# Gated mix of a recurrent memory transformer and a channel MLP: seven deferred tiles, a root of third order, and the first tile's projections behind the last block

## The chip, the cores and the metric

The kernel runs on one core of one Trainium2 chip. The metric is the time of one execution in device microseconds; the median of three runs is 767.43 us (767.12 to 767.94). The profile is of one further execution, with a trace of every instruction.

## The reference

The output mixes two branches of the same input x (2048 tokens of 512, bf16) with a gate per token.

```python
def _A_ref(x, mem0, Wq, Wk, Wv, Wo, seg_len):      # recurrent memory attention
    ...
    mem = mem0                                      # 8 memory tokens
    for s in range(n_seg):                          # 64 segments of 32 tokens
        xs = x[:, s * seg_len:(s + 1) * seg_len, :].copy()
        h = jnp.concatenate([mem, xs], axis=1)
        q = jnp.einsum('btd,dhe->bhte', h, Wq)      # 32 heads of 128
        k = jnp.einsum('btd,dhe->bhte', h, Wk)
        v = jnp.einsum('btd,dhe->bhte', h, Wv)
        ...                                         # masked softmax of q k, times v
        o = jnp.einsum('bhte,hed->btd', o, Wo)
        mem = o[:, :M, :].copy()                    # the next segment needs it
        outs.append(o[:, M:, :])
    return jnp.concatenate(outs, axis=1)

def _B_ref(x, w1, b1, w2, b2):                      # F = 1376
    y = _layernorm(x, axis=-1)
    h = _gelu(jnp.einsum('bsd,df->bsf', y, w1) + b1)
    return jnp.einsum('bsf,fd->bsd', h, w2) + b2

g = _sigmoid((x * gate_w).sum(-1, keepdims=True))
return g * _A_ref(...) + (1 - g) * _B_ref(...)
```

## The kernel before

The 2048 tokens are 16 tiles (T) of 128 tokens; a tile is four segments, and a segment is one step (s = 4 T + si, 64 steps). The kernel has two phases. Every engine runs its instructions in the order in which the program text issues them; there is no scheduler in between (the region is under a manual schedule), so the text's order is each queue's order. Loads of data are DMAs issued from a queue: most from SP (`nc.sync`), a few from ScalarE (`nc.scalar`) and GpSimd (`nc.gpsimd`).

**First phase, the MLP.** It runs over 8 blocks of two tiles. A block has 11 units (fc), one for each 128 columns of F. `a_mm` (L464) computes one unit: four matmuls of 256 columns into bank SbF or W in turn, and a Gelu on ScalarE with the bias `b1_sb` into `hTm`. `b_mm` (L471) follows two units later (LAG) and multiplies the unit by w2 into the output bank of each tile, one 512-column matmul per tile. `prep` (L422) normalizes the next block's two tiles on VectorE; blocks after the first take the inverse root from `rsqrt` (L410), a bit trick with three Newton rounds on [128 x 2] values. `prep_tr` (L443) transposes the normalized tiles through X1 and X2. `gates` (L455) makes the gate and its complement `omg`, by which the finished block is scaled while it is evicted (`ct_out`, L493) and stored in DRAM (`c_dr`). While this goes on, the attention's weights arrive: `loads` (L351) issues two pieces of Wv, Wq or Wk in each of blocks 0 to 5, and Wo in block 6.

The tiles in `DEF` (L67) are deferred: their Gelu result is not multiplied by w2 here. `spill` (L484) writes it to DRAM (`h_dr`) in two pieces, and the second phase reads it back.

The start of the phase: 13 matmuls on an identity (`warm`, L519), the first two tiles' statistics, their transposes, two more such matmuls, the transpose of the bias (L529) through bank W with its copy to `b1_sb`, and then the units. In the last block `first` (L511) is spread between the units 5, 7 and 9: it projects the last 8 tokens of each segment of tile 0 to Q, K and V, in six parts of 16 matmuls each on quarter-width tiles (`left_qk`, `left_v`), through X1, X2 and U[0].

**Second phase, the steps.** A step projects 32 rows (24 tokens of its segment and the 8 memory rows) to Q, K and V (L127, L146), computes scores (`scores`), exponentials, the products with V (`av`, L289 and L294), and one pass of Wo for the rows of the step (`wo_pass`, L158), out of which `new_mem` (L728) takes the next memory. The last 8 tokens of each segment ("left") are projected a tile ahead as filler: `side` (L615) returns a generator of such work for each step, and `run(n)` and a few single calls put its items into the step's text where TensorE would wait. An item is four quarter-width matmuls of 512 columns. For the last tile there is no next tile, so `side` is empty there but for step 62.

The deferred tiles are another filler: `mlp_halves` (L653) reads one spilled unit `hm` and multiplies it by w2 in two halves of four quarter-width matmuls of 256 columns into bank W; two halves stand in each step (L805 and L814), and step 2 has seven units more. `hm_load` (L633) issues the load of a unit on SP, four ahead, into five buffers; it is called at the second half of a unit. `hm_load4` loads four units in one DMA, at step 2.

The softmax's normalization of the rows goes through DRAM: `recip_x` (L694) writes reciprocals to `r_dr` on SP and reads them back broadcast as `Rb` on SP. GpSimd's `x_norm` (L707) multiplies by Rb in the next step and writes UT, which `wo_pass` of that step reads.

At the border of the phases the tiles of the second phase (UT, QT, KT, E and others) take over the memory of the first, so their first writers wait for the last readers of what was there, the spills of hTm among them.

Of the kernel before, what the change touches and what calls it, by code (L numbers as in the profile page):

```python
# [10 lines left out]
BF16 = mybir.dt.bfloat16  # L11
I32 = mybir.dt.int32
ACTF = mybir.ActivationFunctionType
ALU = mybir.AluOpType
# [9 lines left out]
RSQRT_SEED = 0x5F3759DF  # L24
# [3 lines left out]
def kernel(ctx, tc, A_x, A_mem0, A_Wq, A_Wk, A_Wv, A_Wo, A_seg_len, B_x, B_w1, B_b1, B_w2, B_b2, gate_w, out):  # L28
# [38 lines left out]
    DEF = (1, 3, 5, 9, 11, 13)  # L67
# [232 lines left out]
    with tc.tile_pool(name="mlpw", bufs=1) as mlpw, \  # L300
# [35 lines left out]
        nc.sync.dma_start(w1_sb[:, :, F0:F1], w1v[:, :, F0:F1])  # L336
        nc.sync.dma_start(w1_sb[:, :, F1:F], w1v[:, :, F1:F])
        nc.gpsimd.dma_start(gw_bc[:], gate_w.partition_broadcast(P))
        nc.sync.dma_start(w2_sb[:, H2:FC - 1, :], B_w2[H2 * P:(FC - 1) * P, :].rearrange("(fc p) d -> p fc d", p=P))
# [70 lines left out]
        def rsqrt(y, v, n):  # L410
            i1 = msmall.tile([P, n], I32, tag="i1", name="i1")
            nc.vector.tensor_scalar(out=i1[:], in0=v.bitcast(I32), scalar1=1, scalar2=None, op0=ALU.logical_shift_right)
            nc.vector.tensor_scalar(out=y.bitcast(I32), in0=i1[:], scalar1=-1, scalar2=RSQRT_SEED, op0=ALU.mult, op1=ALU.add)
            for _ in range(3):
                t = msmall.tile([P, n], FP32, tag="nt", name="nt")
                nc.vector.tensor_tensor(out=t[:], in0=y, in1=y, op=ALU.mult)
                nc.vector.scalar_tensor_tensor(out=t[:], in0=t[:], scalar=-0.5, in1=v, op0=ALU.mult, op1=ALU.mult)
                nc.vector.scalar_tensor_tensor(out=y, in0=t[:], scalar=1.5, in1=y, op0=ALU.add, op1=ALU.mult)
# [3 lines left out]
        def prep(blk):  # L422
            mv = msmall.tile([P, TB, nc.vector.BN_AGGR_DIM], FP32, tag="mv", name="mv")
            ve = msmall.tile([P, TB], FP32, tag="ve", name="ve")
            rs = msmall.tile([P, TB], FP32, tag="rs", name="rs")
            for tt in range(TB):
                st = msmall.tile([P, nc.vector.BN_STATS_DIM], FP32, tag="st", name="st")
                nc.vector.bn_stats(out=st[:], in_=xts[blk * TB + tt][:])
                nc.vector.bn_aggr(out=mv[:, tt, :], in_=st[:])
            nc.vector.tensor_scalar(out=ve[:], in0=mv[:, :, 1], scalar1=LN_EPS, scalar2=None, op0=ALU.add)  # L430
            if blk == 0:
                nc.scalar.activation(out=rs[:], in_=ve[:], func=ACTF.Sqrt)
                nc.scalar.activation(out=dummy[:], in_=ident[:, 0:1], func=ACTF.Gelu_apprx_tanh)
                nc.vector.reciprocal(out=rs[:], in_=rs[:])
            else:
                rsqrt(rs[:], ve[:], TB)
            for tt in range(TB):
                T = blk * TB + tt
                ys[T] = mwork.tile([P, Dm], BF16, tag="y", name="y")
                nc.vector.tensor_scalar(out=ys[T][:], in0=xts[T][:], scalar1=mv[:, tt, 0:1], scalar2=rs[:, tt:tt + 1], op0=ALU.subtract, op1=ALU.mult)  # L440
            yTs[blk] = mwork.tile([P, KC, TB * P], BF16, tag="yT", name="yT")
# [13 lines left out]
        def gates(blk):  # L455
            t0, t1 = blk * TB, blk * TB + TB
            nc.scalar.activation(out=th[:, t0:t1], in_=z_all[:, t0:t1], func=ACTF.Tanh, scale=0.5)
            nc.vector.tensor_scalar(out=g_all[:, t0:t1], in0=th[:, t0:t1], scalar1=0.5, scalar2=0.5, op0=ALU.mult, op1=ALU.add)
# [5 lines left out]
        def a_mm(blk, fc):  # L464
            rows = min(P, F - fc * P)
            hp = (SbF, W)[(blk * FC + fc) % 2]
            for kc in range(KC):
                nc.tensor.matmul(hp[:rows, 0:TB * P], lhsT=w1_sb[:, kc, fc * P:fc * P + rows], rhs=yTs[blk][:, kc, :], start=(kc == 0), stop=(kc == KC - 1))  # L468
            nc.scalar.activation(out=hTm[blk % 2][:rows, fc, :], in_=hp[:rows, 0:TB * P], func=ACTF.Gelu_apprx_tanh, bias=b1_sb[:rows, fc:fc + 1], scale=1.0)
# [41 lines left out]
        def first():  # L511
            bks = (X1, X2, U[0], X1, X2, U[0])
# [11 lines left out]
        b1p = W[:].bitcast(BF16)[:, 0:FC]  # L524
# [3 lines left out]
        warm(2)  # L528
        nc.tensor.transpose(b1p, b1r[:], ident[:FC, :FC])  # L529
        nc.vector.tensor_copy(out=b1_sb[:], in_=b1p)  # L530
# [3 lines left out]
        for n, (blk, fc) in enumerate(units):  # L534
# [33 lines left out]
            elif fc >= 1:  # L568
                if fc == 2:
                    spill(blk - 1, 6, FC)  # L570
                if fc == 1:
                    side0 = first()
                if fc == 3:
                    gates(blk)
                for _ in range((0, 0, 0, 0, 0, 8, 0, 8, 0, 8, 0)[fc]):
                    next(side0, None)
                    flush(act_q, 9)
                    flush(dve_q, 9)
        for n in range(len(units) - LAG, len(units)):
            b_mm(*units[n])  # L580
        for _ in side0:
            flush(act_q, 9)
            flush(dve_q, 9)
# [69 lines left out]
    def mlp_halves():  # L653
        while hms:
            T, fc, hm, n = hms.pop(0)
            for h in range(2):
# [4 lines left out]
                if h == 1:  # L661
                    hm_load(n)
# [9 lines left out]

    hm_load(4)
# [20 lines left out]
    def recip_x(s):  # L694
# [4 lines left out]
        nc.sync.dma_start(r_dr[s % 2][:], R[:, 8 * NG:RW])  # L699
        nc.sync.dma_start(Rb[:].rearrange("p r e -> p (r e)"), r_dr[s % 2][:].rearrange("r e -> (r e)").partition_broadcast(P))  # L700
# [33 lines left out]
    for s in range(nseg):  # L734
# [18 lines left out]
        if s == 2:  # L753
            hm_load4()
# [49 lines left out]
        if not last:  # L804
            next(mlp, None)  # L805
# [8 lines left out]
        next(mlp, None)  # L814
# [200 lines left out]
```

## Time and profile before

| what | us |
|---|---|
| median of three runs | 767.43 |
| the profiled execution's own time | 767.13 |
| its span, first to last instruction | 765.4 |
| TensorE matmuls busy | 744.7 (97%) |
| TensorE weight loads busy | 423.4 (55%) |
| ScalarE busy | 537.1 (70%) |
| VectorE busy | 401.0 (52%) |
| GpSimd busy | 275.1 (36%) |

The granted TensorE clock is 0.998 over the span. The first phase ends and step 0 begins at 86 us; the rest are the 64 steps and a short tail.

How to read the rows: an engine is PE (TensorE), PEld (its weight loads), ACT (ScalarE), DVE (VectorE), POOL (GpSimd) or SP (SyncE); a trailing q means the engine's sequencer, which issues DMAs. L127 is a line of the kernel. "out<-in" names tiles, xN counts instructions that are merged into the row. In a timeline a row has its start in us from the span's start, its length, and in brackets the idle time of the engine before it and what ended it. A matmul's length is that from its issue to its modelled end; matmuls overlap, so the distance from start to start is what one costs. A list of waits has the engine and line that waited, what released it, the total in us, how often, and the longest. A row of stretches has the stretch, its length, busy time and count for PE, PEld, DVE, ACT and POOL, then the granted clock, the mean busy share of the 16 DMA engines, and GB/s.

### The profile page before, as it was taken

Reading aid. Unit: us, or ns where it says so; the run is one execution under the profiler, and the core shown is the slowest. Engines: PE = TensorE matmul, PEld = TensorE weight load, DVE = VectorE, ACT = ScalarE, POOL = GpSimd, SP = SyncE. Lnnn points to the kernel's source line nnn. Section 1 sums busy time; section 2 is a strip of 40 time slices with the busy share of each in tenths; the row PEclk is TensorE's granted clock in tenths of the full one; section 3 lists DMA queues with packets and bytes.
Section 4 is the critical chain, followed back from the end, with each engine's and each line's share of the span. In section 5 each row is a group of like instructions: output and inputs, shape, how many; then the busy total and the mean of one; then the engine's idle time right before and its main releaser. Section 6 shows DMA issues by size and latency. Waiting matters only on the chain.

```text
span 765.4 us, 44786 instructions
## 1 busy us (share of the span) xinstructions
PE 744.7 (97%) x19624; PEld 423.4 (55%) x19635; DVE 401.0 (52%) x1434; ACT 537.1 (70%) x1625; POOL 275.1 (36%) x517
## 2 busy tenths in 40 slices
PE   8999999999999999999999999999999999999997
PEld 5666455556555555655555655555555555555553
DVE  5876454545555544645455545445454555445444
ACT  4766676777777777777777777777777777677663
POOL 4001133344433334342444333343433444333441
PEclk9999999999999999999999999999999999999999
DMA  8999423212132322222121324222222213222211
GB/s 276 335 305 314 138 76 87 71 59 76 58 94 74 91 66 59 74 83 83 60 78 56 94 66 95 69 56 76 82 78 72 73 56 93 64 83 69 73 57 49
DMA packets 71994, 74.96 MB, mean 98 GB/s; under 512 B 39401, under 2 KB 61906, under 8 KB 70258
## 3 DMA queue, kind: packets, MB, share of 16 engines
q1 hardware_dynamic: 70354, 69.96, 30.1%
q8 instruction: 155, 2.54, 1.4%
q0 software_dynamic: 496, 1.18, 0.5%
q10 hardware_dynamic: 944, 0.92, 0.4%
q14 instruction: 45, 0.37, 0.2%
HBM read 59.13 MB, written 6.62 MB: 86 GB/s over the span
## 4 chain that ended last, share of the span: by engine, by line
PE 93%; DVE 3%; DMA 2%; issue 1%; ACT 1%; SPq 0%; DVEq 0%; ACTq 0%
PE U L127 33%; PE X L158 19%; PE X L146 16%; PE X L127 4%; PE U L289 3%; PE W L468 2%; PE U L475 2%; PE W L659 2%; PE U L146 2%; PE SbF L468 2%; PE U L265 1%; DMA w_sb<-in_B_w_dram 1%; PE U L728 1%; PE SbF L265 1%; PE SbF L685 1%
## 5 line engine op out<-in xcount | busy, mean ns | idle before, releaser
L712 POOL TENSOR_TENSOR UT<-XR,Rb 128x384 bf16<-128x384 bf16 x126 | 140.3, 1137 | 302.0 <-DMA Rb<-r_dr 234.0
L132 ACT CAST Tb<-U 128x512 bf16<-128x512 f32 x288 | 169.0, 587 | 81.7 <-PE U L127 79.1
L127 PEld LDWEIGHTS <-hT 128*32 128x32 bf16 x4096 | 109.5, 96 | 98.7 <-DVE hT L730 8.2
L146 PE MATMUL X<-Wv_sb,hT 128*32 128x512 bf16 x2048 | 144.1, 378 | 0.1
L127 PE MATMUL U<-Wq_sb,hT 128*32 128x512 bf16 x2048 | 137.1, 381 | 0.1
L127 PE MATMUL U<-Wk_sb,hT 128*32 128x512 bf16 x2048 | 133.5, 379 | 0.0
L158 PE MATMUL X<-Wo_sb,UT 128*32 128x512 bf16 x2016 | 122.7, 380 | 1.5 <-ACT UT L819 0.8
L730 DVE CAST hT<-U 128x8 bf16<-128x8 f32 x126 | 21.0, 167 | 168.3 <-PE U L728 126.1
L790 ACT CAST V<-X 128x256 bf16<-128x256 f32 x256 | 88.7, 372 | 16.4 <-PE X L146 3.5
L136 DVE STREAM_TRANSPOSE QT<-Tb 128x256 f32<-128x256 f32 x128 | 56.6, 442 | 73.2 <-ACT Tb L132 72.8
L158 PEld LDWEIGHTS <-UT 128*32 128x32 bf16 x2080 | 56.5, 96 | 60.7 <-issue 17.8
L691 ACT CAST XR<-U 128x256 bf16<-128x256 f32 x252 | 78.4, 433 | 0.0
L719 ACT CAST w<-X 128x128 bf16<-128x128 f32 x189 | 44.7, 309 | 43.6 <-PE X L158 43.6
L136 DVE STREAM_TRANSPOSE KT<-Tb 128x256 f32<-128x256 f32 x128 | 57.0, 445 | 31.1 <-ACT Tb L132 23.2
L712 POOL TENSOR_TENSOR UL<-XR,Rb 128x128 bf16<-128x128 bf16 x126 | 60.5, 504 | 0.0
L146 PEld LDWEIGHTS <-hT 128*32 128x32 bf16 x2048 | 47.1, 94 | 20.5 <-issue 0.2
L704 POOL TENSOR_TENSOR racc<-racc,R 128x72 f32<-128x72 f32 x63 | 21.3, 337 | 102.3 <-DVE R L702 82.1
L819 ACT CAST UT<-U 128x64 bf16<-128x64 f32 x252 | 35.3, 226 | 28.9 <-PE U L294 28.9
L468 PEld LDWEIGHTS <-w_sb 128*128 128x128 bf16 (+1 forms) x352 | 33.3, 100 | 18.6 <-issue 5.5
L773 ACT ACTIVATE E<-U 128x64 bf16<-128x64 f32 (+1 forms) x128 | 35.0, 273 | 11.3 <-PE U L269 11.2
L728 PEld LDWEIGHTS <-w 128*32 128x32 bf16 x1008 | 23.7, 93 | 31.9 <-ACT w L719 25.3
L127 PE MATMUL U<-Wk_sb,GL 128*32 128x512 bf16 x496 | 39.9, 377 | 0.0
(169 smaller groups left out, 1233.3 us busy)
## 6 DMA issues: line engine op xcount, KB each, us to landing
Rb<-r_dr SPq DMA_DIRECT2D x63, 512.0 KB, 4.0
Wv_sb<-in_A_Wv_dram SPq DMA_DIRECT2D x4, 1024.0 KB, 7.4
Wq_sb<-in_A_Wq_dram SPq DMA_DIRECT2D x4, 1024.0 KB, 8.2
Wk_sb<-in_A_Wk_dram SPq DMA_DIRECT2D x4, 1024.0 KB, 8.6
Wo_sb<-in_A_Wo_dram SPq DMA_DIRECT2D x4, 1024.0 KB, 11.1
VP<-VL SPq DMA_DIRECT2D x64, 64.0 KB, 3.3
c<-c_dr SPq DMA_DIRECT2D x16, 128.0 KB, 2.7
hm<-h_dr SPq DMA_DIRECT2D x62, 32.0 KB, 3.3
```

Source lines behind the costliest of these rows:

```text
L127: nc.tensor.matmul(bk[32 * j:32 * j + 32, :], lhsT=G[:, kc, :], rhs=W5[t][:, kc, h0:h1, j, :], start=(kc == 0), stop=(kc == KC - 1), tile_ ...
L132: nc.scalar.copy(out=Tb[:], in_=bk.rearrange("p (a b e) -> p a e b", a=8, b=2))
L136: nc.vector.transpose(out=dst[:, 8 * hf:8 * hf + 8, c0:c0 + 32, :].rearrange("p a r b -> p a (r b)").bitcast(FP32), in_=Tb[:].rearrange("p ...
L146: nc.tensor.matmul(bk[32 * j:32 * j + 32, :], lhsT=G[:, kc, :], rhs=Wv5[:, kc, 4 * vb:4 * vb + 4, j, :], start=(kc == 0), stop=(kc == KC - ...
L158: nc.tensor.matmul(bk[32 * c:32 * c + 32, :], lhsT=U_[:, j, i, :], rhs=Wo_sb[:, 4 * i + j, :], start=(n == 0), stop=(n == NW - 1), tile_po ...
L468: nc.tensor.matmul(hp[:rows, 0:TB * P], lhsT=w1_sb[:, kc, fc * P:fc * P + rows], rhs=yTs[blk][:, kc, :], start=(kc == 0), stop=(kc == KC - 1))
L691: nc.scalar.copy(out=XR[:, j], in_=U[j][:, 0:NG * 40].rearrange("p (i q) -> p i q", q=40)[:, :, 0:32])
L712: nc.gpsimd.tensor_tensor(out=out[:, :, 4 * h:4 * h + 4, o:o + b - a], in0=XR[:, :, 4 * h:4 * h + 4, a:b], in1=Rb[:, h, :, :, a:b], op=ALU ...
L719: nc.scalar.copy(out=w[:, a:b], in_=bk[:, a:b])
L773: nc.scalar.activation(out=E[:, 4 * i2:4 * i2 + 4, c], in_=Sb[i2][:, :, c], func=ACTF.Exp, scale=scale)
L790: nc.scalar.copy(out=V[:, i0:i0 + 2, :].rearrange("p i e -> p (i e)"), in_=(X1, X2)[vb][:, 256 * h:256 * h + 256])
L819: nc.scalar.copy(out=UT[s % 2][:, j, :, 0:M], in_=U[j][:, 0:NG * 40].rearrange("p (i q) -> p i q", q=40)[:, :, 32:40])
```

## The change

- `DEF` gets tile 15. Its Gelu result is spilled in the last block (two more spills on SP), its eleven 512-column matmuls of `b_mm` go, and its 11 units join the filler: `side` gives `mlp_units(4)` in steps 60 and 61, `hm_load4` is called at step 60 too, step 0 has no halves any more, and step 2 has eight units instead of seven.
- `hm_load` is no longer called at the second half of a unit. The number owed is counted, and `recip_x` issues the loads between the write of r_dr and the read of Rb.
- The root has two rounds, one of three and one of four instructions, with other constants; a scale is folded into the addition of epsilon.
- `gates` makes only `omg` in each block; `g_all` is made once, in the last block.
- `first` comes behind the last unit of the last block, in three portions of eight items, with the two lagging `b_mm` calls behind the first portion. It uses U[1] beside X1, X2 and U[0].
- The second piece of w1 is issued ahead of x tiles 2 and 3. The second piece of w2 moves from ScalarE's queue to SP's, behind these. Twelve matmuls instead of 13 and one instead of two are issued at the start, and the bias transpose and its copy move behind the matmuls of the first unit.

```diff
-RSQRT_SEED = 0x5F3759DF
+RSQRT_SEED, RSQRT_A, RSQRT_B = 0x5F1FFFF9, 2.38924456, 0.703952253
+RSQRT_K = 0.375 * RSQRT_B
...
-    DEF = (1, 3, 5, 9, 11, 13)
+    DEF = (1, 3, 5, 9, 11, 13, 15)
...
-        NWARM = 13
+        NWARM = 12
         H1, H2, F1 = 3, 6, 7 * P
-        for a, b in ((0, H1), (H1, H2)):
-            nc.scalar.dma_start(w2_sb[:, a:b, :], B_w2[a * P:b * P, :].rearrange("(fc p) d -> p fc d", p=P))
+        def ld_w2(eng, a, b):
+            eng.dma_start(w2_sb[:, a:b, :], B_w2[a * P:b * P, :].rearrange("(fc p) d -> p fc d", p=P))
+        ld_w2(nc.scalar, 0, H1)
+        nc.sync.dma_start(w1_sb[:, :, F0:F1], w1v[:, :, F0:F1])
         ld_x(2)
         ld_x(3)
-        nc.sync.dma_start(w1_sb[:, :, F0:F1], w1v[:, :, F0:F1])
+        ld_w2(nc.sync, H1, H2)
         nc.sync.dma_start(w1_sb[:, :, F1:F], w1v[:, :, F1:F])
...
-            for _ in range(3):
+            for c, a in ((-1.0, RSQRT_A), (-RSQRT_B * RSQRT_B, 5.0)):
                 t = msmall.tile([P, n], FP32, tag="nt", name="nt")
                 nc.vector.tensor_tensor(out=t[:], in0=y, in1=y, op=ALU.mult)
-                nc.vector.scalar_tensor_tensor(out=t[:], in0=t[:], scalar=-0.5, in1=v, op0=ALU.mult, op1=ALU.mult)
-                nc.vector.scalar_tensor_tensor(out=y, in0=t[:], scalar=1.5, in1=y, op0=ALU.add, op1=ALU.mult)
+                nc.vector.scalar_tensor_tensor(out=t[:], in0=t[:], scalar=c, in1=v, op0=ALU.mult, op1=ALU.mult)
+                if a == 5.0:
+                    nc.vector.scalar_tensor_tensor(out=t[:], in0=t[:], scalar=10.0 / 3.0, in1=t[:], op0=ALU.add, op1=ALU.mult)
+                nc.vector.scalar_tensor_tensor(out=y, in0=t[:], scalar=a, in1=y, op0=ALU.add, op1=ALU.mult)
...
-            nc.vector.tensor_scalar(out=g_all[:, t0:t1], in0=th[:, t0:t1], scalar1=0.5, scalar2=0.5, op0=ALU.mult, op1=ALU.add)
+            if blk == NBLK - 1:
+                nc.vector.tensor_scalar(out=g_all[:], in0=th[:], scalar1=0.5, scalar2=0.5, op0=ALU.mult, op1=ALU.add)
...
+            if blk == 0 and fc == 0:
+                b1p = W[:].bitcast(BF16)[:, 0:FC]
+                nc.tensor.transpose(b1p, b1r[:], ident[:FC, :FC])
+                nc.vector.tensor_copy(out=b1_sb[:], in_=b1p)
...
-            bks = (X1, X2, U[0], X1, X2, U[0])
+            bks = (X1, X2, U[0], U[1], X1, X2)
...
-                if fc == 1:
-                    side0 = first()
                 if fc == 3:
                     gates(blk)
-                for _ in range((0, 0, 0, 0, 0, 8, 0, 8, 0, 8, 0)[fc]):
-                    next(side0, None)
-                    flush(act_q, 9)
-                    flush(dve_q, 9)
-        for n in range(len(units) - LAG, len(units)):
-            b_mm(*units[n])
-        for _ in side0:
-            flush(act_q, 9)
-            flush(dve_q, 9)
+                if fc == 7:
+                    spill(blk, 0, 6)
+        spill(NBLK - 1, 6, FC)
+        side0 = first()
+        for n in range(3):
+            if n == 1:
+                for m in range(len(units) - LAG, len(units)):
+                    b_mm(*units[m])
+            for _ in range(8):
+                next(side0, None)
+                flush(act_q, 9)
+                flush(dve_q, 9)
...
-            gens = [wo_left(T - 1, X1) if T >= 1 else mlp_units(7)]
-        elif T + 1 < NT:
+            gens = [wo_left(T - 1, X1) if T >= 1 else mlp_units(8)]
+        elif T + 1 == NT:
+            gens = [mlp_units(4)] if si < 2 else []
+        else:
...
-                    hm_load(n)
+                    owed[0] += n
...
         nc.sync.dma_start(r_dr[s % 2][:], R[:, 8 * NG:RW])
+        hm_load(owed[0])
+        owed[0] = 0
         nc.sync.dma_start(Rb[:].rearrange("p r e -> p (r e)"), r_dr[s % 2][:].rearrange("r e -> (r e)").partition_broadcast(P))
...
-        if s == 2:
+        if s in (2, (NT - 1) * SPT):
             hm_load4()
...
         if not last:
-            next(mlp, None)
+            if s:
+                next(mlp, None)
...
         run(W1)
-        next(mlp, None)
+        if s:
+            next(mlp, None)
```

More of the change, by code (lines that the diff above doesn't have):

```diff
@@ L429, in prep @@
                 nc.vector.bn_aggr(out=mv[:, tt, :], in_=st[:])
[L430 removed]
+            nc.vector.tensor_scalar(out=ve[:], in0=mv[:, :, 1], scalar1=LN_EPS, scalar2=1.0 if blk == 0 else 1.0 / (RSQRT_K * RSQRT_K), op0=ALU.add, op1=ALU.mult)
             if blk == 0:
@@ L527 @@
             prep_tr(0, tt)
-        warm(2)
-        nc.tensor.transpose(b1p, b1r[:], ident[:FC, :FC])
-        nc.vector.tensor_copy(out=b1_sb[:], in_=b1p)
+        warm(1)
         side0 = iter(())
```

4 lines of the change are left out of this document (2 added, 2 removed).

## The prediction

> **What bounds the kernel now.** The page comes first: its span, the shares of the chain that ended last, and one queue.
>
> ```profile
> span 765.4 us, 44786 instructions
> ...
> PE 744.7 (97%) x19624; PEld 423.4 (55%) x19635; DVE 401.0 (52%) x1434; ACT 537.1 (70%) x1625; POOL 275.1 (36%) x517
> ...
> q8 instruction: 155, 2.54, 1.4%
> ...
> PE 93%; DVE 3%; DMA 2%; issue 1%; ACT 1%; SPq 0%; DVEq 0%; ACTq 0%
> ```
>
> The chain is 93% TensorE, so time is won by taking instructions from TensorE or by ending a wait of TensorE, and nowhere else. Its waits, longest first (us in total, times, longest):
>
> ```profile
> PE U L289 <- issue: 4.1, 10, 0.6
> ...
> PE W L468 <- ACT hTm L469: 1.4, 2, 1.0
> PE W L659 <- DMA hm<-h_dr: 1.2, 1, 1.2
> ...
> PE SbF L468 <- ACT hTm L469: 0.7, 2, 0.5
> PE W L468 <- DMA w_sb<-in_B_w_dram: 0.6, 1, 0.6
> PE X L447 <- DVE y L440: 0.5, 1, 0.5
> ```
>
> Four of these are what the change touches: the hm wait, the w_sb wait and the wait of a transpose for y (L447). The chain in order of time (start, length) then tells a step's length, because each L127 row opens one step.
>
> ```profile
> 84.72 1.30 PE U L475 x6
> 86.01 2.73 PE U L127 x48
> ...
> 97.65 3.69 PE U L127 x68
> ...
> 108.02 3.55 PE U L127 x64
> ...
> 705.69 3.55 PE U L127 x64
> ...
> 715.92 3.55 PE U L127 x64
> ...
> 726.14 3.51 PE U L127 x64
> ...
> 736.30 3.51 PE U L127 x64
> ```
>
> Step 0 takes 97.65 - 86.01 = 11.6 us, step 1 10.4. Steps 59, 60 and 61 take 10.23, 10.22 and 10.16. Step 59 still carries the 32 matmuls of the next tile's V; steps 60 and 61 carry no such filler and are no shorter. So the last tile's steps are set by their own chain of engines and have room for about 32 matmuls (8 x 0.217 us = 1.7 us of TensorE). One full-width 512-column matmul costs 1.30 / 6 = 0.217 us, and four quarter-width ones side by side cost the same.
>
> **The change part by part.** The sum is made against the profiled execution: span 765.4, its time 767.13, so 1.7 lie around the span. The runs' median, 767.43, is 0.3 above it.
>
> *Start.* The second piece of w1 is issued ahead of the x tiles, the second piece of w2 moves from ScalarE's queue to SP's behind them, two warming matmuls go, and the bias transpose moves behind the first unit. From the timeline (start, length, engine, line, what, idle time before and its releaser):
>
> ```profile
> 2.69 0.48 SPq L336 DMA_DIRECT2D w_sb<-in_B_w_dram  x1
> ...
> 7.56 0.76 DVE L448 COPY yT<-X 128x512 bf16<-128x512 bf16 x2 [0.71 <-PE X L447]
> ...
> 8.11 0.18 PE L529 MATMUL W<-ident,b1r 11*128 11x11 bf16 x1
> ...
> 8.37 0.60 PE L468 MATMUL SbF<-yT,w_sb 128*128 128x256 bf16 x4
> ...
> 9.44 0.47 ACT L469 ACTIVATE hTm<-W,b_sb 128x256 bf16<-128x256 f32 x1
> ...
> 9.96 0.38 PE L475 MATMUL U<-w_sb,hTm 128*128 128x512 bf16 x1
> ...
> 10.99 0.61 PE L468 MATMUL W<-yT,w_sb 128*128 128x256 bf16 x4 [0.65 <-DMA w_sb<-in_B_w_dram]
> ```
>
> Unit 3 waits until 10.99 for the w1 piece issued at 2.69. Its two other conditions are met by 10.18 (9.96 + 0.217, and the Gelu from bank W ends at 9.91). The missing warming matmul lets the transposes and unit 0 start some 0.4 earlier. But unit 1 writes bank W, through which the bias transpose now passes after unit 0 (transpose, semaphore, copy: 8.11 to about 8.5, 0.4 us), so unit 1 stays near 8.8. What is left is the load: two x tiles and 384 KB fewer are ahead of it, more than the 0.8 us it is late. I take -0.85; the ends are 0 (it lands as late as now) and -0.95. The pieces pushed back (x tiles, w2) are needed later; if one is late it eats into this term.
>
> *Root and gates.* Two of eleven small VectorE instructions go from each root (3 x 3 + 2 becomes 3 + 4 + 2), and one of two in the gates of seven blocks. The timeline where block 6 ends:
>
> ```profile
> 62.58 0.17 DVE L458 TENSOR_SCALAR g_all<-th 128x2 f32<-128x2 f32 x1 [0.27 <-ACT th L457]
> ...
> 62.66 0.16 DVE L459 TENSOR_SCALAR omg<-th 128x2 f32<-128x2 f32 x1
> ...
> 67.14 0.16 DVE L418 SCALAR_TENSOR_TENSOR rs<-nt,rs 128x2 f32<-128x2 f32 x1
> ...
> 67.33 0.73 DVE L440 TENSOR_SCALAR y<-xt,mv,rs 128x512 bf16<-128x512 bf16 x2
> ...
> 68.20 0.38 PE L447 MATMUL X<-ident,y 128*128 128x128 bf16 x4 [0.49 <-DVE hT L506]
> ```
>
> One root instruction takes 0.19 from start to start (67.14 to 67.33), so y comes 0.39 sooner; that matters only where a transpose waits, in two blocks with 0.5 each (the L447 row of the list of waits, and the 0.49 at 68.20): -0.8 (0 to -1.0). A gate instruction costs 0.08 (62.58 to 62.66). The omg behind it releases the scaled eviction on ScalarE, which holds up the Gelus, and for these TensorE waits 1.4 + 0.7 us in four places: 4 x 0.08 = -0.3 (0 to -0.6). In the other blocks both are hidden by TensorE's own work.
>
> *Tile 15 deferred.* Eleven 512-column matmuls leave the last block: 11 x 0.217 = -2.4. With one output matmul per unit instead of two, the last block becomes like the other deferred ones, which wait for a Gelu near their third unit (2.1 / 4 = 0.5 each): +0.4. The floor is -1.9, and -2.4 is the ceiling. The first tile's projections stay 24 groups of four; they only move behind the last block, where the Gelu tail and the Exp table load are covered by their 5 us.
>
> Added on SP: two spills of tile 15 (352 KB), behind the Wo loads and ahead of the VP load, the ct write, the hm loads and the first r_dr write. The last of them is awaited by the memsets of UT and the first write of QT. Rows of the timeline there, of two stretches, and of the issues (KB, us to landing):
>
> ```profile
> 86.12 1.42 POOL L598 MEMSET UT<- 128x768 bf16 x2 [12.74 <-PE U L475]
> ...
> 87.48 0.42 POOL L248 COPY QT<-QL 128x128 f32<-128x128 f32 x1
> ...
> 89.41 0.27 PE L265 MATMUL SbF<-QT,KT 128*32 128x40 bf16 x16
> ```
>
> ```profile
> 78.00:82.00 4.00, 3.95 (x47) 1.97 (x46) 1.09 (x3) 2.15 (x5) 0.00 (x0) 1.00 1.08 339
> 82.00:86.00 4.00, 4.00 (x47) 1.78 (x50) 1.25 (x4) 2.82 (x5) 0.00 (x0) 1.00 0.06 16
> ```
>
> ```profile
> h_dr<-hTm SPq DMA_DIRECT2D x2, 160.0 KB, 7.9
> ```
>
> The queues are full until 82 (share 1.08) and then empty (0.06); a spill behind Wo took 7.9 us. By the terms so far step 0 starts 3.95 earlier, near 82.0, and its scores need QT 3.4 later (89.41 - 86.01), at 85.4. If the transfers end as late as now, the spills end at 82 + 352 KB / 339 GB/s = 83.0, and QT follows 1.9 later (memsets and copy, 86.12 to 87.90, and a semaphore), at 84.9: covered by 0.5. At half that rate it is 86.0 and step 0 waits 0.6; at a third, 1.6. I take 0, since what stands ahead of Wo's issue moves forward too; ends 0 and +1.6.
>
> *hm.* Step 0 loses its two output halves and with them the wait: -1.2, to about the 10.4 of step 1. The eleven units of tile 15 add 22 halves of 0.11: one unit to step 2 (an empty place there), one to step 59, ten to steps 60 and 61, whose room is 1.7 us each: +0.2, and at most +2.4 if no place is empty. Their loads are issued between the r_dr write and the Rb load; see the fourth rival.
>
> *Pauses before L289.* TensorE pauses ten times, 4.1 us, with no releaser. There are 155 instruction fetches for 19,624 + 19,635 TensorE instructions, one per 253 (the second and third row of the page), so such a pause should fall where a fetch comes late in the dense run of small matmuls. Fewer instructions ahead of the loop shift where the fetches fall in every step. Direction unknown; ends -2 and +2 (half of the 4.1); I take +0.4, since steps 0 and 60 become dense enough to pause too. The Trainium skill ("Runtime: NRT & Kernel Launch", "Instruction fetch mechanics") says that blocks of 256 instructions are fetched ahead and that crossing one is mostly hidden. By that this term would be 0 and the time 0.4 less; the ten pauses speak against "hidden" here.
>
> Sum: -0.85 - 0.8 - 0.3 - 2.4 + 0.4 - 1.2 + 0.2 + 0.4 = -4.55. The profiled time becomes 762.6, and 0.3 more for a median of runs: 762.9.
>
> **The rivals.**
> First, step 0 waits for tile 15's spill: for it the full queues until 82, against it the half microsecond of cover. +1.6: 764.5.
> Second, the fetches fall worse in all 56 middle steps: +2, 764.9.
> Third, the front does not shorten: the start gives 0, the root's waits return behind another VectorE instruction, and only 1.9 + 1.2 remain less 0.6 for the steps: 767.4 - 2.5 = 764.9.
> Fourth, slower. In every step the hm load now stands on SP between r_dr and Rb. The timelines of GpSimd, TensorE and SP in step 58:
>
> ```profile
> 697.43 2.23 POOL L712 TENSOR_TENSOR UT<-XR,Rb 128x384 bf16<-128x384 bf16 x2 [4.39 <-DMA Rb<-r_dr]
> ```
>
> ```profile
> 702.72 1.91 PE L158 MATMUL X<-Wo_sb,UT 128*32 128x512 bf16 x32
> ```
>
> ```profile
> 703.07 0.46 SPq L699 DMA_DIRECT2D r_dr<-R  x1
> 704.68 0.32 SPq L700 DMA_DIRECT2D Rb<-r_dr  x1
> ```
>
> GpSimd waits for Rb, and UT is ready at 699.7 for a use at 702.7: 3.0 of slack; 1.6 lie between r_dr and Rb. An hm issue that is held up more than 4.6 us decides; at 5 us, 56 steps x 0.4 = 22 us, 785. Against it: each load takes a slot that an earlier step has read.
>
> **How the numbers follow.** Forecast 0.66, first rival 0.13, second 0.10, third 0.07, fourth 0.04. The forecast's own range is 761.5 to 764; 760.9 takes in a luckier fetch pattern, 765.2 the first three rivals. A measurement of this kernel tells 0.2% (1.5 us) from no change: faster is below 765.9. The first four cases, 0.96 together, lie there; of these I give 0.08 to no change and 0.01 to slower, for two rivals that come together. Faster 0.87, same 0.08, slower 0.05.
>
> **What would show it.** Right: unit 3 near 10.1 without a wait for w_sb; no wait at L447 over 0.1; step 0's first matmul at 81.5 to 82.8; no wait for hm and step 0 below 10.8; steps 60 and 61 below 10.6. Wrong: a wait of step 0's scores for QT or of POOL's memset for h_dr, Rb issued over 2.5 us after r_dr, or middle steps longer on average than 10.45.

## The result and the profile after

The changed kernel takes 761.36 us (median of 12 runs, 758.08 to 763.62), the kernel before 765.77 (12 runs, 763.15 to 767.94): ratio 0.9942, 95% interval 0.9929 to 0.9955, so 4.4 us faster. The profiled executions are 767.13 and 761.31, 5.8 apart: the one of before was 1.4 above its median, a slow one among its own.

The page after, span, engines and the instruction queue:

```profile
span 759.5 us, 44953 instructions
...
PE 742.4 (98%) x19710; PEld 422.7 (56%) x19710; DVE 398.4 (52%) x1413; ACT 536.7 (71%) x1625; POOL 274.7 (36%) x517
...
q8 instruction: 156, 2.56, 1.4%
```

The rows of TensorE's timeline before that mark the stages (start, length, what, idle time before it and its releaser):

```profile
85.94 1.05 PE L127 MATMUL U<-Wq_sb,hT 128*32 128x512 bf16 x16
...
92.73 0.29 PE L659 MATMUL W<-w_sb,hm 128*32 128x256 bf16 x4 [1.23 <-DMA hm<-h_dr]
...
97.71 0.39 PE L127 MATMUL U<-Wq_sb,hT 128*32 128x512 bf16 x4
```

The same view after, around step 0:

```profile
81.37 1.04 PE L128 MATMUL U<-Wq_sb,hT 128*32 128x512 bf16 x16
...
85.45 0.28 PE L266 MATMUL SbF<-QT,KT 128*32 128x40 bf16 x16 [0.45 <-POOL QT L249]
...
92.36 0.39 PE L128 MATMUL U<-Wq_sb,hT 128*32 128x512 bf16 x4
```

And after, from step 60 on:

```profile
709.36 1.11 PE L128 MATMUL U<-Wq_sb,hT 128*32 128x512 bf16 x16
...
716.19 0.19 PE L295 MATMUL U<-E,VP 32*128 32x64 bf16 x2
716.93 0.20 PE L295 MATMUL U<-E,VP 32*128 32x64 bf16 x2 [0.56 <-issue]
...
720.32 1.05 PE L128 MATMUL U<-Wq_sb,hT 128*32 128x512 bf16 x16
...
740.64 0.66 PE L128 MATMUL U<-Wq_sb,hT 128*32 128x512 bf16 x8
```

Before, the same marks are 715.77 (step 60) and 746.34 (step 63). Each step begins with its first matmul of Wq and hT, so the differences split the span:

| stretch | before | after | change |
|---|---|---|---|
| start to step 0 | 85.94 | 81.37 | -4.57 |
| step 0 | 11.77 | 10.99 | -0.78 |
| steps 1 to 59 | 618.05 | 617.00 | -1.05 |
| steps 60 to 62 | 30.57 | 31.28 | +0.71 |
| step 63 and the end | 19.02 | 18.89 | -0.13 |
| span | 765.36 | 759.53 | -5.83 |

So the first phase brought more than the whole measured gain. Its terms are in TensorE's timeline before and after (unit 3, the block starts that wait for a Gelu, the transposes). Before:

```profile
10.99 0.61 PE L468 MATMUL W<-yT,w_sb 128*128 128x256 bf16 x4 [0.65 <-DMA w_sb<-in_B_w_dram]
...
20.48 0.60 PE L468 MATMUL W<-yT,w_sb 128*128 128x256 bf16 x4 [1.00 <-ACT hTm L469]
...
28.80 0.60 PE L468 MATMUL SbF<-yT,w_sb 128*128 128x256 bf16 x4 [0.46 <-ACT hTm L469]
...
55.94 0.60 PE L468 MATMUL W<-yT,w_sb 128*128 128x256 bf16 x4 [0.44 <-ACT hTm L469]
```

After:

```profile
10.17 0.60 PE L476 MATMUL W<-yT,w_sb 128*128 128x256 bf16 x4
...
19.64 0.60 PE L476 MATMUL W<-yT,w_sb 128*128 128x256 bf16 x4 [0.93 <-ACT hTm L481]
...
27.86 0.60 PE L476 MATMUL SbF<-yT,w_sb 128*128 128x256 bf16 x4 [0.39 <-ACT hTm L481]
...
54.42 0.60 PE L476 MATMUL W<-yT,w_sb 128*128 128x256 bf16 x4 [0.38 <-ACT hTm L481]
...
65.71 0.38 PE L487 MATMUL U<-w_sb,hTm 128*128 128x512 bf16 x1
66.19 0.38 PE L454 MATMUL X<-ident,y 128*128 128x128 bf16 x4
```

Unit 3 starts 0.82 sooner and waits for no load. Each wait for a Gelu is 0.06 to 0.07 shorter (1.00 to 0.93, 0.46 to 0.39, 0.44 to 0.38). The transposes of block 6, before which TensorE idled 0.49 at 68.20, now start at 66.19, 0.10 after the end of the matmul before them (65.71 + 0.38).

### The profile page after: what moved, and what is told of

It is laid out like the page before. It is cut to its first block, busy times and chain, and to the rows that moved or that the text cites. A ratio compares the mean times of both kernels' runs of the same rounds, so it can differ in the third digit from the quotient of the medians.

```text
span 759.5 us, 44953 instructions
## 1 busy us (share of the span) xinstructions
PE 742.4 (98%) x19710; PEld 422.7 (56%) x19710; DVE 398.4 (52%) x1413; ACT 536.7 (71%) x1625; POOL 274.7 (36%) x517
## 4 chain that ended last, share of the span: by engine, by line
PE 87%; issue 1%; ACT 0%; DVE 0%; POOL 0%; DVEq 0%
PE U L128 33%; PE X L159 19%; PE X L147 17%; PE X L128 4%; PE U L290 3%; PE W L671 2%; PE U L147 2%; PE U L266 1%; PE U L743 1%; PE SbF L266 1%; PE SbF L698 1%; PE U L295 1%; PE U L277 1%; PE W L159 0%; PE U L280 0%
## 5 line engine op out<-in xcount | busy, mean ns | idle before, releaser
L128 PEld LDWEIGHTS <-hT 128*32 128x32 bf16 x4096 | 107.6, 96 | 100.8 <-DVE hT L745 8.5
L159 PE MATMUL X<-Wo_sb,UT 128*32 128x512 bf16 x2016 | 121.1, 380 | 0.0
L147 PEld LDWEIGHTS <-hT 128*32 128x32 bf16 x2048 | 46.8, 94 | 20.8
L159 PE MATMUL X<-Wo_sb,UL 128*32 128x512 bf16 x512 | 39.4, 379 | 0.8 <-issue 0.8
```

The costliest lines, as they stand in the source:

```text
L128: nc.tensor.matmul(bk[32 * j:32 * j + 32, :], lhsT=G[:, kc, :], rhs=W5[t][:, kc, h0:h1, j, :], start=(kc == 0), stop=(kc == KC - 1), tile_ ...
L147: nc.tensor.matmul(bk[32 * j:32 * j + 32, :], lhsT=G[:, kc, :], rhs=Wv5[:, kc, 4 * vb:4 * vb + 4, j, :], start=(kc == 0), stop=(kc == KC - ...
L159: nc.tensor.matmul(bk[32 * c:32 * c + 32, :], lhsT=U_[:, j, i, :], rhs=Wo_sb[:, 4 * i + j, :], start=(n == 0), stop=(n == NW - 1), tile_po ...
```

## The experiments

Three sets ran, each on one chip with the kernel before beside it: 763.87 us in the set of the padded kernels, 763.20 in the second set, 763.82 in the third. Times are therefore compared within a set. Of the three, the changed kernel itself ran in the third only, and ratios do not carry over well: all four kernels of the second set take 611 to 614 us for the steps 1 to 59, all the others 615 to 618. The stretches of every profiled execution, from the same marks as in the table above (the first two rows are the kernels of the result; set 1: the padded kernels; set 2: front_old, no15, hm_old, spillq; set 3: after_again, the changed kernel once more, and the rest):

```
                  step 0    step 0   steps    steps    step 63   median us, and ratio to
                  starts    takes    1 to 59  60 to 62 and end   the kernel before (95%)
before             85.94     11.77   618.05    30.57    19.02
after              81.37     10.99   617.00    31.28    18.89    0.9942 (0.9929 to 0.9955)
front_old          83.54     10.43   614.25    30.99    19.42    759.07  0.9939 (0.9919 to 0.9958)
no15               83.31     10.35   614.07    30.84    19.36    759.13  0.9937 (0.9919 to 0.9954)
hm_old             81.32     11.46   611.17    31.39    18.42    757.74  0.9926 (0.9911 to 0.9940)
spillq             81.15     11.02   612.35    31.44    18.50    756.69  0.9912 (0.9893 to 0.9930)
after_again        81.53     10.35   616.07    31.95    18.56    760.03  0.9937 (0.9915 to 0.9959)
first_in           82.09     10.83   615.54    31.65    18.38    759.57  0.9945 (0.9924 to 0.9965)
no15_first_in      83.65     11.58   615.99    30.54    19.43    762.23  0.9975 (0.9960 to 0.9990)
spill_hm           82.65     10.97   617.67    31.02    18.85    760.49  0.9948 (0.9929 to 0.9967)
pad256             81.87     11.35   615.36    31.23    19.30    760.21  0.9953 (0.9937 to 0.9970)
pad56              81.40     11.66   615.89    30.86    18.45    759.96  0.9955 (0.9938 to 0.9972)
pad136             81.53     10.35   618.11    31.39    18.94    762.23  0.9988 (0.9975 to 1.0001)
pad16              81.54     11.48   614.82    30.57    21.76    761.51  0.9972 (0.9958 to 0.9986)
```

**The front undone.** Against the changed kernel:

```diff
-        nc.sync.dma_start(w1_sb[:, :, F0:F1], w1v[:, :, F0:F1])
+        ld_w2(nc.scalar, H1, H2)
         ld_x(2)
         ld_x(3)
-        ld_w2(nc.sync, H1, H2)
+        nc.sync.dma_start(w1_sb[:, :, F0:F1], w1v[:, :, F0:F1])
...
-            for c, a in ((-1.0, RSQRT_A), (-RSQRT_B * RSQRT_B, 5.0)):
+            for _ in range(3):
...
-            if blk == NBLK - 1:
-                nc.vector.tensor_scalar(out=g_all[:], in0=th[:], scalar1=0.5, scalar2=0.5, op0=ALU.mult, op1=ALU.add)
+            nc.vector.tensor_scalar(out=g_all[:, t0:t1], in0=th[:, t0:t1], scalar1=0.5, scalar2=0.5, op0=ALU.mult, op1=ALU.add)
```

> The changed kernel with the old start (the order of w1, x and w2, the number of warming matmuls, the place of the bias transpose), the root of three rounds of three instructions, and both gate instructions in each block. Forecast's theory: unit 3 starts 0.85 later (near 11.0, waiting for w_sb), the two transposes of blocks 3 and 6 wait 0.4 longer each (0.65 to 0.7 in place of 0.26 to 0.29), and each wait at a block's start is 0.07 longer, so step 0 starts 2.0 later (83.4). Rival (the front does not set step 0's start, the loads do): step 0 starts within 0.7 of 81.4. Steps 0 to 62 take 658 to 660 in both.

TensorE's timeline of this kernel:

```profile
11.03 0.61 PE L472 MATMUL W<-yT,w_sb 128*128 128x256 bf16 x4 [0.92 <-DMA w_sb<-in_B_w_dram]
...
20.53 0.60 PE L472 MATMUL W<-yT,w_sb 128*128 128x256 bf16 x4 [1.00 <-ACT hTm L473]
...
40.48 0.40 PE L451 MATMUL X<-ident,y 128*128 128x128 bf16 x4 [0.53 <-DVE y L444]
...
68.28 0.38 PE L451 MATMUL X<-ident,y 128*128 128x128 bf16 x4 [0.49 <-DVE hT L510]
```

All three waits are back, and step 0 starts at 83.54, 2.17 later than in the changed kernel: as the forecast's theory has it. But step 0 takes 10.43 in place of 10.99, since its scores no longer wait for QT, so step 1 starts only 1.61 later (2.09 later than in the changed kernel's second execution, whose scores do not wait either). The ratio does not tell it from the changed kernel (0.9939 beside 0.9937 and 0.9942), but those come from other sets. Beside the two kernels of its own set that keep the new front (hm_old and spillq below, 757.74 and 756.69) it is 1.3 and 2.4 us slower, which is the size of the front's gain; the intervals are about as wide.

**Tile 15 not deferred.** Only the list, and what follows from it:

```diff
-    DEF = (1, 3, 5, 9, 11, 13, 15)
+    DEF = (1, 3, 5, 9, 11, 13)
...
-            if s:
-                next(mlp, None)
+            next(mlp, None)
...
-        if s in (2, (NT - 1) * SPT):
+        if s == 2:
```

> The changed kernel without tile 15 in the list of deferred tiles: eleven matmuls are back in the last block, step 0 has its two halves, step 2 seven units, and steps 60 and 61 have none. Forecast's theory (the part is worth 2.4 in the last block less a new wait of 0.4, and about 1 of the hm wait in step 0, less what its units cost): step 0 starts 2.0 to 2.4 later (83.4 to 83.8), it waits about 1 us for hm, its scores wait for nothing, step 60 takes 10.25 in place of 10.95; the time is 2 to 3 us over the changed kernel's, so 1.5 to 2.5 us under the kernel before. Rival (the work is only moved: the matmuls come back in steps 60 and 61 and the spill delays step 0): the time is within 1 us of the changed kernel's.

Step 0 starts at 83.31: 1.94 later, as forecast. The scores wait for nothing, steps 60 to 62 are 0.4 to 1.1 shorter than in the changed kernel's two executions, and the hm wait did not come back: step 0 takes 10.35 with both of its halves in it. So of the 1.94, some 0.4 to 1.1 is given back at the end, and in executions with a wait for QT another 0.6: start, step 0 and steps 60 to 62 together, the deferral is worth 0.7 to 0.9. Outside steps 1 to 59 this kernel takes 143.9 (83.31 + 10.35 + 30.84 + 19.36), the changed one 142.5 and 142.4, but 0.5 and 0.8 of that difference lie in step 63 and the end, which the edit does not touch and which take 18.4 to 19.4 in kernels with and without it. In its own set it is 1.4 and 2.4 us slower than hm_old and spillq, which keep tile 15 deferred. So the gain lies around the rival's 1 us rather than at the forecast's 2 to 3: the work is in good part moved, not saved.

**What ended the hm wait.** Two kernels put the first tile's projections back into the last block, one with tile 15 deferred and one without:

```diff
+                if fc == 1:
+                    side0 = first()
...
+                for _ in range((0, 0, 0, 0, 0, 8, 0, 8, 0, 8, 0)[fc]):
+                    next(side0, None)
...
-        side0 = first()
-        for n in range(3):
-            if n == 1:
-                for m in range(len(units) - LAG, len(units)):
-                    b_mm(*units[m])
...
+        for m in range(len(units) - LAG, len(units)):
+            b_mm(*units[m])
```

> The changed kernel with the first tile's projections back between the units 5, 7 and 9 of the last block, and the two lagging output calls behind the last unit. Forecast's theory (moving them is worth 0): step 0 starts at 81.2 to 81.7 as in the changed kernel. Rival 1 (behind the block they cover the tail of the Gelu): step 0 starts 0.3 to 1.0 later. Rival 2 (in the block they cover the new wait of 0.29 at unit 2 and the Gelus of each unit): 0.3 earlier. ct is evicted later, so the hm loads start some 3 us after step 0's start in place of 1 us or less before; no step uses them before step 1, so no wait comes of it.

> The kernel without tile 15 in the list, and the first tile's projections back in the last block. It tells what ended the hm wait of step 0. Theory M (the move: with the projections behind the lagging output calls, ct is evicted at 79.7, 3.6 before step 0 starts, and the hm loads behind its store on SP start 1.2 after that start; before, 85.8 and 3.2): the wait of TensorE for hm is back, 0.8 to 1.4 us, step 0 takes 11.2 to 11.8, the hm loads start 2.8 us or more after step 0's start. Theory H (the forecast: the two halves left out of step 0 ended it; something else, the loads of the first phase, ended it in the kernel without tile 15): no hm wait, step 0 at 10.3 to 10.5.

Without tile 15 and with the projections behind the block (the kernel above), the timeline of VectorE, SP and TensorE has:

```profile
79.74 1.41 DVE L511 TENSOR_SCALAR ct<-U,omg 128x512 bf16<-128x512 f32 x2 [8.20 <-PE U L487]
...
80.52 2.41 SPq L512 DMA_DIRECT2D c_dr<-ct  x2
...
83.31 1.04 PE L128 MATMUL U<-Wq_sb,hT 128*32 128x512 bf16 x16
...
84.52 1.75 SPq L650 DMA_DIRECT2D hm<-h_dr  x4
```

With the projections inside the block:

```profile
83.54 1.41 DVE L511 TENSOR_SCALAR ct<-U,omg 128x512 bf16<-128x512 f32 x2 [0.38 <-PE U L487]
...
83.65 1.05 PE L128 MATMUL U<-Wq_sb,hT 128*32 128x512 bf16 x16
...
84.32 1.01 SPq L512 DMA_DIRECT2D c_dr<-ct  x2
...
86.86 3.12 SPq L649 DMA_DIRECT2D hm<-h_dr  x4
...
90.26 0.29 PE L670 MATMUL W<-w_sb,hm 128*32 128x256 bf16 x4 [1.05 <-DMA hm<-h_dr]
```

The four loads stand on SP behind the stores of ct. Behind the block, ct is evicted 3.6 before step 0 starts and the loads issue 1.2 after that start; inside it, ct comes at the start and the loads 3.2 after. That brings back the wait of 1.05 and a step 0 of 11.58. Theory M holds. In the changed kernel the wait is ended twice: by the move alone (no15) and by the missing halves alone (first_in has no hm wait either). The two are worth 1.2 together, not each. In this pair of kernels, where the deferral ends the hm wait too, the whole time shows it: 759.57 with tile 15 deferred, 762.23 without, in one set.

First_in also prices the move itself. Step 0 starts at 82.09, 0.72 and 0.56 later than in the changed kernel's two executions; without tile 15 the same move is worth 0.34 (83.65 and 83.31). The end of the block shows part of it, in TensorE's timeline:

```profile
81.26 0.90 PE L487 MATMUL U<-w_sb,hTm 128*128 128x512 bf16 x2
...
82.09 1.05 PE L128 MATMUL U<-Wq_sb,hT 128*32 128x512 bf16 x16
```

The two last output matmuls take 0.83 from the first to what follows, where two cost 0.43: the last Gelu runs from 81.24 to 81.71, and the second of them needs it. Rival 1 of the expectation is right and the forecast's 0 wrong, by 0.6 to 0.7 us of gain.

**The spill's queue and the place of the hm loads.**

```diff
-                    nc.sync.dma_start(h_dr[T][a:b].rearrange("f p t -> p f t"), src[:, a:b])
+                    (nc.gpsimd if blk == NBLK - 1 else nc.sync).dma_start(h_dr[T][a:b].rearrange("f p t -> p f t"), src[:, a:b])
```

> The changed kernel with the two spills of tile 15 issued on GpSimd's queue instead of SP's, where they stand behind the loads of Wo. If the spill's place behind Wo is what makes step 0's scores wait for QT (85.45 in place of 84.7), the memset of UT starts before 82.5 (83.63 now), the wait of 0.5 for QT is gone and step 0 takes 10.3 to 10.5 in place of 10.99. Rival (the spill lands late because the 16 DMA engines are full until 82, whatever the queue): the memset starts within 0.5 of 83.6 and step 0 stays at 10.8 to 11.2. The whole time moves by 0.7 us at most in both.

```diff
-                    owed[0] += n
+                    hm_load(n)
...
-        hm_load(owed[0])
-        owed[0] = 0
```

> The changed kernel with the hm loads issued where they were, at the second half of a unit, and not between the r_dr write and the Rb load. Forecast's theory: no effect, as r_dr to Rb is 1.55 before and 1.59 changed: steps 0 to 62 take 657.5 to 660, the time is within 0.2%. Rival (the issue between the two delays Rb and so some steps): steps 0 to 62 are 1.5 us or more shorter.

With the spill on GpSimd's queue (timeline of all engines):

```profile
81.15 1.04 PE L128 MATMUL U<-Wq_sb,hT 128*32 128x512 bf16 x16
...
82.50 1.42 POOL L608 MEMSET UT<- 128x768 bf16 x2 [5.61 <-DMA c_dr<-ct]
...
84.60 0.27 PE L266 MATMUL SbF<-QT,KT 128*32 128x40 bf16 x16
...
89.35 1.70 PE L159 MATMUL X<-Wo_sb,UT 128*32 128x512 bf16 x28 [0.49 <-issue]
```

The memset starts at 82.50 in place of 83.63, and the scores wait for nothing. The releaser in the row is a transfer that landed near by; in eleven of the fourteen profiles the memset starts 0.22 to 0.27 after the landing of the last spill (83.36 in the changed kernel; 82.28 here, and that is tile 13's second piece, still on SP). Yet step 0 takes 11.02: 0.88 pass at 88.47 in a pause without a releaser. The pause is not new with the edit, as the kernel with the old hm loads has both, QT's wait and a pause of 0.69 at that place, in a step of 11.46. The two places of the hm loads cannot be told apart: 63 issues from r_dr to Rb have a median of 1.57 with the old place, 1.59 with the new and 1.55 before.

Both edits together:

> The changed kernel with the spills of tile 15 on GpSimd's queue and the hm loads at the second half of a unit. Theory that both add up (QT's wait of 0.6 in step 0 goes, the hm loads' place does nothing): 0.5 to 1 us under the changed kernel. Rival (a pause before L159 in step 0 takes the place of QT's wait, 0.82 with the spill moved and 0.48 to 0.62 without): the same time as the changed kernel within 0.4 us, step 0 at 10.9 to 11.2.

This was no better than the changed kernel beside it (760.49 and 760.03). In this execution TensorE waited 1.3 us for w_sb in two places of the first phase, so step 0 started at 82.65, though the front is the changed kernel's. The lower ratio of the spill alone (0.9912) did not return. It came from the second set, where all kernels had short steps 1 to 59, so no version here is shown to beat the changed kernel.

**The changed kernel again.**

> The changed kernel itself, unchanged, so that the other three stand beside it on the same chip. On the chip of the run without tile 15, the kernel before took 763.2 and steps 0 to 62 of four kernels took 654 to 656, on the first chip 659. If the differences in steps 3 to 58 belong to the chip and the execution, and not to the edits, this kernel is 4 to 6 us under the kernel before and its steps 0 to 62 are within 1.5 us of those of the three others of this set, but for steps 0, 60 and 61.

Step 0 takes 10.35 without any wait for QT and step 60 11.36. Steps 1 to 59 are not within 1.5 us of the others: 615.5, 616.1 and 617.7 in kernels with the same stream of TensorE instructions there, 611.2 and 612.4 in set 2, 617.0 in the first profile. One stream of TensorE instructions gives 6.5 us of difference over 59 steps, and the two edits in hm_old and spillq do not explain it: spill_hm has both and the longest steps. The end of the next experiment shows where the time goes.

**Pauses and the boundaries of 256 instructions.** Tiny matmuls among the warming ones shift TensorE's whole stream:

```diff
-        warm(NWARM)
+        warm(NWARM - 1)
+        for k in range(29):
+            c = slice(32 * (k % 4), 32 * (k % 4) + 32)
+            nc.tensor.matmul(U[3][c, 0:4], lhsT=ident[:, c], rhs=ident[:, 0:4], start=True, stop=True, skip_group_check=True, tile_position=(0, 32 * (k % 4)))
```

Each matmul is two instructions, so this is a shift of 56; the others differ in the two numbers.

> The changed kernel with 132 tiny matmuls (32 rows, 4 columns) among the warming ones at the start and four warming ones fewer: 256 instructions more (132 x 2 - 4 x 2) in TensorE's stream ahead of unit 0, a whole block of 256. Theory F (TensorE pauses where its stream crosses a boundary of 256 instructions, if the 256 before it ran in less than some 3.5 us): no step changes, steps 0 to 62 take 659.3 us as in the changed kernel within what executions differ, and pauses fall in the same steps (37, 54, 39, 30, 60). Rival N (the pauses have nothing to do with the count of instructions, they come from other traffic): steps 0 to 62 take 659.3 as well; in both the start may be up to 1 us later by the tiny matmuls themselves. This run is the control for the other three.

> As the control, but 29 tiny matmuls and one warming one fewer: 56 instructions more. Theory F: the boundaries move 56 instructions forward in the code of every step, that is back into its denser part; by the intervals of 256 instructions in steps without a pause the pauses of steps 3 to 58 grow from 10.3 to 17.7 us, of which 4 to 7.5 is felt: steps 0 to 62 take 663 to 667 us, the time is 0.5 to 1.0% over the changed kernel's. Rival N: 659.3, the same time.

> As the control, 70 tiny matmuls and two warming ones fewer: 136 instructions more. Theory F: pauses of steps 3 to 58 grow from 10.3 to 18.4 us, 4 to 8 of it felt: steps 0 to 62 take 663 to 667. Rival N: 659.3.

> As the control, 9 tiny matmuls and one warming one fewer: 16 instructions more. Theory F: pauses of steps 3 to 58 fall from 10.3 to 7.6 us, 1.5 to 2.7 of it felt: steps 0 to 62 take 656.6 to 657.8. Rival N: 659.3.

Every weight load has its record, so each can be given its number in the program's stream. The next table takes the boundaries (instruction 192 of each 256, numbered from the kernel's first) within steps 3 to 58, and counts where five instructions took over 0.4 us. Beside it stands the mean of the same count at the 15 other offsets of 16 that a boundary could have had, where the 256 instructions before took under 3.4 us. The estimate is the one behind the expectations: each boundary pauses for what the 256 instructions before it, in steps without a pause, lack of 3.46 us:

```
kernel         pauses   their    by the     at another offset
               at 130   sum us   estimate   (mean)
before           18      10.9      10.0      0.6, 0.3 us
after            10       7.4      10.3      0.6, 0.3 us
pad256            9       6.3      10.3      0.5, 0.2 us
pad56            11       8.3      17.7      0.6, 0.3 us
pad136           16      11.2      18.4      0.7, 0.3 us
pad16             7       3.9       7.6      0.7, 0.3 us
```

The place is settled: pauses sit at the boundaries and go with them when the stream is shifted. The pause in step 60 (716.19) is at instruction 192, after 256 that took 2.5 us, and it returns at that matmul in other executions (0.96 in the changed kernel's second one, 0.72 with the spill moved). The size did not come as expected: the padded kernels come in the expected order, at about half of it, and steps 0 to 62 take 657.9, 658.4, 659.9 and 656.9 where 659, 663 to 667, 663 to 667 and 656.6 to 657.8 were expected. Theory F fails on the two that were to be slow by 4 or more; only the shift of 136 is slower than its control (0.9988 beside 0.9953), by 2 us of median. The shift of 16 has the fewest pauses and the shortest steps but no shorter time: its profiled execution lost 2.9 us behind the start of step 63. Of these, 0.82 is a wait of TensorE for GpSimd's UL, and 2.1 lie before TensorE's very last instruction, which starts at 760.13 when the other engines have ended by 757.99.

What the pauses wait for can be read from the same traces, since they hold every transfer of the instruction queue q8: 155 to 157 of 16 KB in a profile, one for each 256 instructions of TensorE (157 where 256 instructions were added), each 0.9 to 2.4 us long in steps 1 to 59. Taken in order, every boundary has its transfer: for the pause in step 60 shown above it runs from 714.44 to 715.39, and TensorE stands from 716.17 to 716.93. In steps 1 to 59 of all fourteen profiles there are 144 pauses, and after each TensorE goes on 1.19 to 1.65 us after the end of its boundary's transfer. At the 1787 boundaries without a pause TensorE never goes on sooner than 1.19 after it, and at half of them it comes 2.4 or more after it. So a pause is the wait for the fetched block, and it depends on when the block arrives as well as on how fast the code before it ran; the estimate with its fixed 3.46 us left out when it arrives. The late last instruction of the shift of 16 fits: a transfer ends 1.46 before it. Why some transfers come later than others was not followed.

The 6.5 us by which one stream varies are these waits. In seven kernels the instructions of steps 1 to 59 are the same and stand at the same places between the boundaries. For each, the time from one weight load to the next is set against the median of the eleven profiles with these instructions, and the excess is summed, once for the loads numbered 188 to 204 of each 256 and once for all others:

```
              steps      excess at        excess
              1 to 59    the boundaries   elsewhere
hm_old        611.17     1.7              1.8
spillq        612.35     3.3              1.4
pad256        615.36     5.3              2.4
first_in      615.54     5.4              2.5
after_again   616.07     6.1              2.3
after         617.00     7.5              1.9
spill_hm      617.67     8.1              1.9
```

The order is the same, and 6.4 of the 6.5 us lie at the boundaries.

## Why the prediction was right

- **Start, -0.85.** Measured 0.82, by the cause that was named. It is not certain in every execution: of twelve profiles with the new front, one waited 1.3 us for w_sb, in part at unit 3 again, and two waited 0.23 for a later piece of w2.
- **Root, -0.8.** 0.39 at each of two transposes (idle of 0.49 and 0.10 at the one in block 6).
- **Gates, -0.3.** 0.06 to 0.07 at each block start that is shown, some 0.3 over five of them (from front_old to the changed kernel), where four of 0.08 were counted.
- **Tile 15, -2.4 and +0.4.** 1.94 at the start of step 0 (no15), beside 2.0. Its two terms are less exact than their sum: the new wait for a Gelu, counted with 0.4, is 0.12 (at 70.87); what takes up the rest was not followed.
- **First tile's projections, 0.** Wrong: 0.6 to 0.7 gained (first_in). This is why step 0 starts at 81.37, just ahead of the 81.5 to 82.8 that were named.
- **Spill behind Wo, 0.** The first rival's wait came in part: 0.45 idle for QT in the profile shown. Of eight profiled executions with this spill order and this front, four had it. The spill's last piece landed at 83.36 and the memset started at 83.63, where the estimate put the spill's end at 83.0; and step 0 came earlier than estimated, so the half microsecond of cover was used up.
- **hm, -1.2.** The wait is gone and the term's size was right, but the reason was one of two that each suffice.
- **Units of tile 15, +0.2.** Steps 61 and 62 take 10.15 and 10.17, so nothing is seen there. Step 60 is 0.7 longer by its pause.
- **Pauses, +0.4.** The range of 2 both ways held, the value means little: steps 1 to 59 were 1.05 shorter in this pair, and one stream varies by 6.5. The cause that was named, a fetch that comes late in dense code, is what the transfers show, though by the forecast it was argued and not yet shown. "Steps 0 and 60 become dense enough to pause too" was right in its place, and the pauses are larger than the whole 0.4 where they come: 0.7 in step 60 here and 1.1 in the second execution, 0.7 or more in step 0 of six other kernels.
- **Fourth rival.** Nothing of it: Rb is issued 1.59 after r_dr (median; 1.55 before). Single issues come up to 3.9 after it, and up to 3.1 before the change.

The sum, -4.55, stands beside a measured -4.4, closer than it deserves: two errors cancel in it, 0.6 too little for the first phase, and about as much too little for QT's wait and the pauses of steps 0 and 60. What the two profiles show beyond it, 1.05 in steps 1 to 59, is less than one stream varies by. That the median of the runs came within 0.2 us of the sum is luck where pauses alone move an execution by 6. The predicted 762.9 is 1.5 over the measured 761.36 because it was counted from three runs (767.43) that lie 1.7 above the median of twelve. Of the marks named, several failed though the time came out: step 0 takes 10.99 where below 10.8 was named (10.35 in the second execution), step 60 takes 10.95 where below 10.6 was named, and the scores' wait for QT was a mark of being wrong. "Middle steps longer on average than 10.45" was badly set: steps 3 to 58 average 10.47 after the change, and 10.49 before it.

## What to carry to other kernels

Where TensorE sets the time, gains of single waits are read exactly from the starts of stages, long before the whole time can tell them; but each has to be followed to the next thing that arrives late, since in one execution 0.6 of the front's 2.2 us was handed to a spill that lands at a time of its own. When two edits each end the same wait, undoing one shows nothing: undo both. Put the unchanged kernel into every set: without it a set in which all kernels happen to take less looks like a gain of its edits. And a profile of one execution is a poor basis for an absolute time where the same instructions take 6 us more or less; counting the instructions between the late places, and looking up the transfer that each boundary needs, told here why.

## What the hardware showed that was not expected

Dense code of small matmuls pauses where TensorE's stream crosses a boundary of 256 instructions: 7 to 18 pauses of 0.4 to 1.4 us at some 130 boundaries in the six kernels of the table, in each kernel all but at most three of them where the 256 before ran in under 3.4 us. Each pause ends 1.19 to 1.65 us after the 16 KB instruction transfer of that boundary has ended, so it is the wait for it, and the arrival of these transfers varies enough to make 6 us of difference between executions of the same instructions. The Trainium skill ("Runtime: NRT & Kernel Launch", "Instruction fetch mechanics") has such crossings mostly hidden; that holds at over 85% of the boundaries here, and the pauses at the rest add up to 4 to 11 us. Shifting the stream moves the pauses and changes their sum, but it did not shorten the kernel.
